# Attention scores as eight independent 64x32 float32 tiles of the TensorE array, instead of split or zero-padded full-array products

## The chip, the cores and the metric

One core of one Trainium2 chip runs the whole program. The metric is device time in microseconds (us) of one execution; three runs of the kernel before gave 707.91, 707.54 and 706.74, median 707.54. The engines are TensorE (PE in the profile, its weight loads PEld), VectorE (DVE), ScalarE (ACT), GpSimd (POOL) and SyncE (SP), which issues most of the DMAs. Each engine works through its own instructions in the order of the built program and waits on semaphores for the others.

## The reference

Eight batches, eight heads, 512 tokens and 32 memory slots per head, head width 64. Both attentions share one score matrix and its transpose; the result goes through a feed-forward layer of 2048 with a squared ReLU.

```python
B, H, S, Ns, D = (8, 8, 512, 32, 64)
scores  = scale * x @ state^T              # (B, H, 512, 32)
a       = softmax(scores);   xread = a  @ state
scores2 = scale * state @ x^T              # the transpose of scores
a2      = softmax(scores2);  sread = a2 @ x
x   = concat([xread, sread], axis=2) -> (B * 544, 512)
out = relu(x @ w_in) ** 2 @ w_out          # d_ff = 2048
```

All of it is float32.

## The kernel before

**The feed-forward part is most of the work.** For each batch the 2048 hidden units are taken in 16 chunks of 128. `mlp` makes for each chunk an `up` (six products of 128x512, tile `ph`, line 392) and a `down` (twelve products, tiles `po`, line 418). The state is folded into `w_in` beforehand: `z` = state times w_in (tile `pz`, line 191 plain, line 203 split), so that `up` multiplies `z` directly with the attention weights `a`. Large products are not done in float32: an operand is split into a high part, rounded to the type `fp32r` (a cast on ScalarE), and a low part (a subtraction on VectorE or GpSimd), both by the helper `split` (lines 97 and 98). Three fp32r products, or two, stand for one in float32.

**The scores of a batch** come in two groups of four heads (`NG` = 2, `HG` = 4). A group has two pairs of heads (`q`). For a pair, 128 rows of `xT` hold both heads' 64 dimensions, and the stationary operand holds the two heads' states in the two diagonal blocks of a matrix that is zero elsewhere, so that one product gives both heads' 32 scores each.

- For the first two batches (`b < PLAIN_X`) the products are plain float32 (line 298): the state is copied into the zeroed `sp_f` (line 250, ScalarE), and two products accumulate into the tile `pst` in PSUM.
- From batch 2 on (line 288), `x` is split into `xt_hl` (`cut_t`: ScalarE, then GpSimd) and the state into `sp_hl` (`pad`: ScalarE, then VectorE). The state's high and low parts stand beside each other as 128 stationary columns, so two products per pair suffice. The lower half of the result (`pq[2N:]`) is copied to SBUF by ScalarE (`st_low`, line 293) and added to the upper half by VectorE (`st`, line 294).

Then both softmaxes run from the scores: a 32x32 transpose and a row maximum on VectorE (lines 303 and 305), the exponentials on ScalarE.

**PSUM.** The pool `ps_x` has two buffers with the tag `px`, for `pst` or `pq`, `pz`, the transposes `pt` and the reads `pr`.

**Products of 64 rows.** At the start of the program TensorE has several plain `pz` products of 64 rows; `pz_361` lies in the array's rows 64 to 127 and `pz_411` in rows 0 to 63:

```order
L191 MATMUL pz_355<-wf_268,st_f_169 128x256 x2
L392 MATMUL ph_231<-a_lo_108,z_hi_232 128x512
L392 MATMUL ph_312<-a_lo_108,z_hi_232 128x512
L191 MATMUL pz_361<-wf_268,st_f_169 128x256 x2
L191 MATMUL pz_411<-wf_285,st_f_169 128x256 x2
```

The two products of `pz_361` stand before the two of `pz_411`; each is two records in the trace.

**What sets the order.** Attention, the `z` products and the weight conversions are cut into steps. `Ahead.run`, called twice per chunk from `mlp`, emits as many steps as their due time asks for; `lags` keeps a step a slot behind what it needs. Within that order a scheduler places the instructions of each engine by its own simulation of the time, so that a step's products may stand apart on TensorE, with `ph` and `po` products between them. The steps of a batch's scores are listed in `order(b)`.

Of the kernel before, what the change touches and what calls it, by code (L numbers as in the profile page):

```python
# [9 lines left out]
F32 = mybir.dt.float32  # L10
F32R = mybir.dt.float32r
# [7 lines left out]
def memory_attention_then_relu2_ffn(  # L19
# [21 lines left out]

    nc = tc.nc
    P = 128
    B, C, S = xT.shape
    D = stT.shape[1]
    H = C // D
    N = stP.shape[2] // (H // 2)
    DM, DF = w_out.shape[1] // 2, w_out.shape[0]
    R = S + N
    NG = H * N // P  # L50
    HG = H // NG
# [5 lines left out]
    FPC = FW // P  # L57
    GB = P // N
    NGB = B // GB
# [1 line left out]
    assert math.frexp(SCALE)[0] == 0.5  # L61
    EPS = 1e-9
    RAW = 4
    XRAW = 2
    PLAIN_Z = 6
    PLAIN_X = 2
    BOTH = ((0, 6), (1, 10), (0, NFC), (1, NFC))
    LATE = 3

# [3 lines left out]
    const = ctx.enter_context(tc.tile_pool(name="const", bufs=1))  # L73
    sb = ctx.enter_context(tc.tile_pool(name="sb", bufs=2))
# [3 lines left out]
    ps_x = ctx.enter_context(tc.tile_pool(name="ps_x", bufs=2, space=bass.MemoryType.PSUM))  # L78
# [2 lines left out]
    make_identity(nc, ident)  # L81

    wo = [None] * NFCH
    sp_hl = const.tile([P, NG, 2, 2, 2 * N], F32R, name="sp_hl")
    nc.gpsimd.memset(sp_hl.bitcast(F32), 0.0)
    sp_f = const.tile([P, NG, 2, P + D], F32, name="sp_f")
    nc.gpsimd.memset(sp_f, 0.0)
    sr = [const.tile([P, C], F32, name=f"sr{i}") for i in range(NGB)]

    wd = [dr.tile([P, NCC, FW], F32, name=f"wd_{k}") for k in range(NFCH)]  # L90
    zd, st, z_first = {}, {}, []
# [31 lines left out]
    def z_state(G):  # L123
        if G == 0:
            raw = sb.tile([P, H, GB * N], F32, name="st_f", tag="x_hl", bufs=1)
            st["raw"] = raw
        else:
            raw = sb.tile([P, H, GB * N], F32, name="st_raw", tag="raw", bufs=RAW)
        for j in range(2):
            nc.sync.dma_start(out=raw[j * D:(j + 1) * D].rearrange("d h m -> d (h m)"), in_=stT[G])  # L130
        hi = sb.tile([P, H, GB * N], F32R, name="stz_hi", bufs=1)
        lo = sb.tile([P, H, GB * N], F32R, name="stz_lo", bufs=1)
        if G:
            split(hi, lo, raw, nc.gpsimd)
# [102 lines left out]


    def attention(b):
        pair = []  # L240

        def pad():
            pair.extend(sb.tile([P, NG, S], F32R, name=n, bufs=2) for n in ("a_hi", "a_lo"))
            raw = sb.tile([P, NG, 2, N], F32, name="sp_raw", bufs=2)
            nc.sync.dma_start(out=raw.rearrange("p g q n -> p (g q n)"), in_=stP[b])
            for i in range(2):
                rows = slice(i * D, (i + 1) * D)
                at = slice(i * N, (i + 1) * N)
                if b < PLAIN_X:
                    nc.scalar.copy(out=sp_f[rows, :, :, at], in_=raw[rows])  # L250
                    continue
                split(sp_hl[rows, :, :, 0, at], sp_hl[rows, :, :, 1, at], raw[rows], nc.vector)

        return pair, pad, [attention_group(b, g, pair) for g in range(NG)]

    def attention_group(b, g, pair):
        CG = C // NG
        NQ = CG // P
        NJ = S // 32
        my = {}  # L260

        def load_t():
            my["t"] = sb.tile([P, NQ, S], F32, name="xt_raw", tag="xraw", bufs=XRAW)
            nc.sync.dma_start(
                out=my["t"], in_=xT[b, g * CG:(g + 1) * CG, :].rearrange("(q p) s -> p q s", p=P)
            )

        def load_n():
            my["n"] = sb.tile([P, NT, CG], F32, name="xn_raw", tag="xraw", bufs=XRAW)
# [1 line left out]
                out=my["n"], in_=xn[b, :, g * CG:(g + 1) * CG].rearrange("(t p) c -> p t c", p=P)  # L271
            )

        def cut_t():
            if b < PLAIN_X:
# [6 lines left out]
        def scores():  # L282
            if b >= PLAIN_X:
                pst = sb.tile([P, S], F32, name="st", bufs=1)
                for q in range(NQ):
                    pq = ps_x.tile([P, S], F32, name="pq", tag="px")
                    for i, v in enumerate(my["xt"]):
                        nc.tensor.matmul(  # L288
                            pq, lhsT=sp_hl[:, g, q].rearrange("p i n -> p (i n)"), rhs=v[:, q, :],
                            start=i == 0, stop=i == 1,  # L290
                        )
# [3 lines left out]
            else:  # L295
                pst = ps_x.tile([P, S], F32, name="pst", tag="px")
                for q in range(NQ):
                    nc.tensor.matmul(
                        pst, lhsT=sp_f[:, g].rearrange("p q n -> p (q n)")[:, q * P:(q + 1) * P],
                        rhs=my["t"][:, q, :], start=q == 0, stop=q == NQ - 1,  # L300
                    )
# [49 lines left out]
        def read():  # L351
# [16 lines left out]
            for q in range(NQ):  # L368
                for i in range(2):
# [4 lines left out]
                        in1=low[i * N:(i + 1) * N, q, i * D:(i + 1) * D],  # L374
                    )

        names = (load_t, cut_t, scores, soft1, soft1b, load_n, cut_n, turn, read)
        return {f.__name__: f for f in names}


# [78 lines left out]
    begins, ends, at = {}, {}, {}  # L459
# [11 lines left out]
    def emit(step):  # L471
        step()
        emitted[step] = slot[0]

    class Ahead:
# [25 lines left out]
    attentions = {b: attention(b) for b in range(B)}  # L501
    a_of = {b: attentions[b][0] for b in range(B)}
    zs = [[z_part(G, k, g) for k in range(NFCH) for g in range(NG)] for G in range(NGB)]
    lags = {}
    for _, _, c, ps in zs[0] + zs[1]:
        lags[ps[0]] = [(c, 2)]
    for b in range(B):
        for g in range(NG):
            w = attentions[b][2][g]
            lags[w["scores"]] = [(w["cut_t"], 1)]  # L510
            lags[w["turn"]] = [(w["scores"], 1)]
            lags[w["read"]] = [(w["turn"], 1), (w["cut_n"], 1)]
            if b:
                lags[w["soft1b"]] = [(w["soft1"], 1)]

    def order(b):
        _, pad, (p, q) = attentions[b]
# [11 lines left out]
    _, pad, (p, q) = attentions[0]  # L529
    z0, z1 = zs  # L530
    for s_ in (
        pad, p["load_t"], q["load_t"], z0[0][0], z0[1][0], p["cut_t"], p["scores"], p["soft1"],
        q["cut_t"], q["scores"], q["soft1"], p["soft1b"], q["soft1b"], lambda: z_state(0),
        z0[0][1], z0[0][2], z0[1][1], z0[1][2], *z0[0][3], *z0[1][3], z0[2][0], z0[3][0],
    ):
        emit(s_)

    weights, reads = Ahead(), Ahead()
    for m in range(NFC):
        steps = []  # L540
# [12 lines left out]
    for m in range(NFC):  # L553
        steps = list(z1[m][3])
# [6 lines left out]
    for b in range(1, B + LATE):  # L561
        steps = order_read(b - LATE) if b >= LATE else []
# [115 lines left out]
```

## Time and profile before

| | |
|---|---|
| runs, median of 3 (lowest to highest) | 707.54 us (706.74 to 707.91) |
| span of the profiled execution | 706.6 us, 9753 instructions |
| TensorE busy | 669.8 us (95%) |
| VectorE / ScalarE / GpSimd busy | 452.2 / 398.3 / 199.3 us |
| DMA | 90.58 MB, mean 128 GB/s |
| chain that ended last | PE 79%, DVE 8%, DMA 6% |

The span is the time from the first to the last instruction of the one profiled execution; the median of the runs is 0.9 us longer. A busy time is the union of an engine's instructions. The ends of matrix products are modelled, so the distance between the starts of two products says what one costs, not the duration in its row. A float32 product stands in the trace as two records, an fp32r product as one. The granted clock (PEclk) is given as a share of 2.4 GHz: 1.00 is that, 0.50 is 1.2 GHz.

### The profile page before, as it was taken

How to read it: one execution, taken by the hardware profiler on the slowest of the kernel's cores; microseconds unless marked ns; L12 is line 12 of the kernel's file. 1: busy time of each engine (PE TensorE's matmuls, PEld its weight loads, DVE VectorE, ACT ScalarE, POOL GpSimd, SP SyncE). 2: the span in 40 equal slices, each digit the busy share in tenths (PEclk: the TensorE clock that was granted, in tenths of full speed). 3: DMA queues.
4: the chain of work that ended last, by engine and by line, in shares of the span. 5: the costliest groups of instructions: out<-in, count | busy, mean ns of one | idle time of the engine just before them, and what ended most of it. 6: DMA issues, size and time to landing. Idle time of an engine off the chain costs nothing.

```text
span 706.6 us, 9753 instructions
## 1 busy us (share of the span) xinstructions
PE 669.8 (95%) x3152; PEld 551.6 (78%) x3152; DVE 452.2 (64%) x757; ACT 398.3 (56%) x727; POOL 199.3 (28%) x181
## 2 busy tenths in 40 slices
PE   4688789999999999999999999999999999999997
PEld 2355668778888888888888878888888888888996
DVE  4859999758456944447945794797944445443553
ACT  3767687567565863467735653665654344332442
POOL 2314433345443540053403240344242022000000
PEclk8589999999999999999999999999999999999999
DMA  8898899435363542344423312412241112100421
GB/s 276 270 315 283 258 306 315 131 97 153 98 202 122 166 149 62 102 135 120 135 78 120 87 48 74 139 58 90 89 150 61 30 31 90 31 16 0 130 80 32
DMA packets 74548, 90.58 MB, mean 128 GB/s; under 512 B 7680, under 2 KB 57600, under 8 KB 74496
## 3 DMA queue, kind: packets, MB, share of 16 engines
q1 hardware_dynamic: 56896, 72.90, 32.9%
q10 hardware_dynamic: 17600, 17.04, 7.1%
q8 instruction: 25, 0.41, 0.3%
q14 instruction: 27, 0.22, 0.1%
HBM read 60.03 MB, written 29.88 MB: 127 GB/s over the span
## 4 chain that ended last, share of the span: by engine, by line
PE 79%; DVE 8%; DMA 6%; issue 2%; ACT 2%; SPq 1%; POOL 0%; DVEq 0%; ACTq 0%; POOLq 0%
PE po L418 47%; PE ph L392 25%; PE pz L203 3%; DMA wo_raw<-w_out 2%; PE pr L355 2%; DMA sp_raw<-stP 2%; PE pq L288 1%; PE pt L343 1%; DVE wf L117 1%; DVE wf L113 1%; DVE z_lo L98 1%; DVE g_lo L98 1%; DMA zd<-z_stage 1%; DMA xt_raw<-xT 1%; DVE wf L109 1%
## 5 line engine op out<-in xcount | busy, mean ns | idle before, releaser
L418 PE MATMUL po<-wo_hi,g_hi 128*128 128x512 f32 x544 | 217.3, 400 | 0.6 <-ACT g_hi L97 0.5
L418 PE MATMUL po<-wo_lo,g_hi 128*128 128x512 f32 x544 | 215.0, 395 | 0.0
L398 DVE TENSOR_TENSOR ph<-ph,r 128x512 f32<-128x512 f32 (+1 forms) x134 | 89.1, 665 | 169.1 <-ACT r L394 168.9
L394 ACT ACTIVATE r<-ph 128x512 f32<-128x512 f32 (+1 forms) x144 | 82.1, 572 | 171.0 <-PE ph L392 169.6
L418 PE MATMUL po<-wo_hi,g_lo 128*128 128x512 f32 x544 | 152.2, 392 | 0.0
L418 PEld LDWEIGHTS po<-wo_hi,g_hi 128*128 128x128 f32 x544 | 103.9, 191 | 22.4 <-ACT g_hi L97 2.0
L418 PEld LDWEIGHTS po<-wo_lo,g_hi 128*128 128x128 f32 x544 | 103.9, 191 | 19.5
L418 PEld LDWEIGHTS po<-wo_hi,g_lo 128*128 128x128 f32 x544 | 101.5, 189 | 21.1 <-issue 1.0
L98 DVE TENSOR_TENSOR g_lo<-ph,g_hi 128x512 fp32r<-128x512 f32 (+1 forms) x144 | 94.4, 656 | 36.3 <-ACT g_hi L97 27.7
L97 ACT CAST g_hi<-ph 128x512 fp32r<-128x512 f32 (+1 forms) x144 | 81.0, 563 | 57.9 <-DVE ph L398 51.7
L392 PE MATMUL ph<-a_hi,z_hi 128*128 128x512 f32 x256 | 81.4, 399 | 2.6 <-DVE nm L306 1.5
L392 PE MATMUL ph<-a_lo,z_hi 128*128 128x512 f32 x256 | 80.1, 392 | 0.0
L392 PE MATMUL ph<-a_hi,z_lo 128*128 128x512 f32 x256 | 80.0, 394 | 0.0
L98 POOL TENSOR_TENSOR xn_hl<-xn_raw,xn_hl 128x1024 fp32r<-128x1024 f32 x16 | 38.9, 2432 | 138.0 <-ACT xn_hl L97 71.2
L182 POOL TENSOR_TENSOR w<-wf,w 64x512 fp32r<-64x512 f32 x32 | 43.0, 1343 | 74.9 <-ACT w L181 69.8
L392 PEld LDWEIGHTS ph<-a_hi,z_hi 128*128 128x128 f32 x256 | 47.6, 190 | 15.2 <-DVE g_lo L98 2.1
L392 PEld LDWEIGHTS ph<-a_hi,z_lo 128*128 128x128 f32 x256 | 48.5, 190 | 10.4
L392 PEld LDWEIGHTS ph<-a_lo,z_hi 128*128 128x128 f32 x256 | 48.2, 189 | 10.5 <-issue 0.3
L98 POOL TENSOR_TENSOR xt_hl<-xt_raw,xt_hl 128x1024 fp32r<-128x1024 f32 x12 | 28.9, 2406 | 75.4 <-ACT xt_hl L97 43.7
L98 DVE TENSOR_TENSOR z_lo<-z_raw,z_hi 128x512 fp32r<-128x512 f32 x64 | 47.9, 750 | 0.3 <-DMA wd<-wf 0.3
L97 ACT CAST z_hi<-z_raw 128x512 fp32r<-128x512 f32 x64 | 39.2, 615 | 1.3 <-DMA wd<-wf 0.8
L98 POOL TENSOR_TENSOR wo_lo<-wof,wo_hi 128x512 fp32r<-128x512 f32 x16 | 25.2, 1578 | 51.4 <-ACT wo_hi L97 51.4
(97 smaller groups left out, 833.7 us busy)
## 6 DMA issues: line engine op xcount, KB each, us to landing
zd<-z_stage ACTq DMA_DIRECT2D x64, 256.0 KB, 3.2
z_raw<-zd SPq DMA_DIRECT2D x252, 64.0 KB, 2.4
xt_raw<-xT SPq DMA_DIRECT2D x16, 512.0 KB, 3.8
w_raw<-w_in SPq DMA_DIRECT2D x16, 512.0 KB, 5.3
wo_raw<-w_out SPq DMA_DIRECT2D x16, 512.0 KB, 5.8
xn_raw<-xn SPq DMA_DIRECT2D x16, 512.0 KB, 3.9
out<-sum SPq DMA_DIRECT2D x32, 256.0 KB, 2.5
wd<-wf SPq DMA_DIRECT2D x16, 256.0 KB, 3.7
```

The costliest lines, as they stand in the source:

```text
L97: nc.scalar.copy(out=hi, in_=src)
L98: eng_lo.tensor_sub(out=lo, in0=src, in1=hi.bitcast(F32))
L109: nc.vector.tensor_scalar(out=bits, in0=bits, scalar1=3, scalar2=0x7FFFFFF8, op0=ALU.logical_shift_left, op1=ALU.bitwise_and,)
L113: nc.vector.scalar_tensor_tensor(out=bits, in0=high, scalar=-0x80000000, in1=bits, op0=ALU.bitwise_and, op1=ALU.bitwise_or,)
L117: nc.vector.scalar_tensor_tensor(out=bits, in0=low, scalar=29, in1=bits, op0=ALU.logical_shift_right, op1=ALU.bitwise_or,)
L182: nc.gpsimd.tensor_sub(out=w[other], in0=wf[own], in1=w[own].bitcast(F32))
L203: nc.tensor.matmul(pz[:, q, :], lhsT=a[:, h, :], rhs=w, start=j == 0, stop=j == len(todo) - 1,)
L355: nc.tensor.matmul(pr[:, q].rearrange("p i c -> p (i c)"), lhsT=my["e"][:, t, q].rearrange("p i n -> p (i n)"), rhs=my["xn"][:, t, q].rear ...
L392: nc.tensor.matmul(ph, lhsT=w, rhs=v, start=i == 0, stop=i == len(todo) - 1)
L394: nc.scalar.activation(r, ph, AF.Relu)
L398: nc.vector.tensor_mul(out=ph, in0=ph, in1=r)
L418: nc.tensor.matmul(po[t], lhsT=g, rhs=w, start=i == 0 and j == 0, stop=i == last and j == 2)
```

## The change

The scores of a batch become one step, `scores`, of eight float32 products. Each has 64 contraction rows and 32 stationary columns, so it takes one of the eight 64x32 tiles of the array: heads 0 to 3 (group 0) lie in partitions 0 to 63, heads 4 to 7 in partitions 64 to 127, and head `j` of a group writes rows `32j` to `32j+31` of that group's `pst`. To allow this, `xT` and `stP` are laid out by halves of heads on the host, as before with other index orders. `pad` only loads the state; `load_a` and `load_b` each load two heads of both halves; `cut_t`, `xt_hl`, `sp_hl`, `sp_f`, `st_low` and `st` are gone. The rest of the old `scores` step is now `exps`, which reads `pst` from PSUM in every batch. `XRAW`, the number of buffers for raw `x`, goes from 2 to 3.

```diff
-    XRAW = 2
+    XRAW = 3
-    sp_hl = const.tile([P, NG, 2, 2, 2 * N], F32R, name="sp_hl")
-    nc.gpsimd.memset(sp_hl.bitcast(F32), 0.0)
-    sp_f = const.tile([P, NG, 2, P + D], F32, name="sp_f")
-    nc.gpsimd.memset(sp_f, 0.0)
...
+        def scores():
+            for g in range(NG):
+                halves[g]["pst"] = ps_x.tile([P, S], F32, name="pst", tag="px")
+            for j in range(HG):
+                x = my["t", j // (HG // 2)][:, j % (HG // 2), :]
+                for g in range(NG):
+                    rows = slice(g * D, (g + 1) * D)
+                    nc.tensor.matmul(
+                        halves[g]["pst"][j * N:(j + 1) * N], lhsT=my["s"][rows, j, :],
+                        rhs=x[rows], start=True, stop=True,
+                    )
...
-        def cut_t():
-            if b < PLAIN_X:
-                return
-            hl = sb.tile([P, 2, NQ, S], F32R, name="xt_hl", tag="x_hl", bufs=1)
-            hi, lo = hl[:, 0], hl[:, 1]
-            split(hi, lo, my["t"], nc.gpsimd)
-            my["xt"] = hi, lo
...
-            if b >= PLAIN_X:
-                pst = sb.tile([P, S], F32, name="st", bufs=1)
-                for q in range(NQ):
-                    pq = ps_x.tile([P, S], F32, name="pq", tag="px")
-                    for i, v in enumerate(my["xt"]):
-                        nc.tensor.matmul(
-                            pq, lhsT=sp_hl[:, g, q].rearrange("p i n -> p (i n)"), rhs=v[:, q, :],
-                            start=i == 0, stop=i == 1,
-                        )
-                    low = sb.tile([2 * N, S], F32, name="st_low", tag="at", bufs=2)
-                    nc.scalar.copy(out=low, in_=pq[2 * N:])
-                    nc.vector.tensor_add(out=pst[q * 2 * N:(q + 1) * 2 * N], in0=pq[:2 * N], in1=low)
...
         return [
-            pad, p["load_t"], p["cut_t"], q["load_t"], p["scores"], p["soft1"], q["cut_t"],
-            q["scores"], p["soft1b"], q["soft1"], q["soft1b"],
+            w["pad"], w["load_a"], w["load_b"], w["scores"], p["exps"], p["soft1"], q["exps"],
+            p["soft1b"], q["soft1"], q["soft1b"],
         ]
```

The order of the instructions changes with it. On TensorE, around the first scores of batch 2, the kernel before has this (`pq` are the scores, `pz` the state times w_in, `po` and `ph` the feed-forward):

```order
L203 MATMUL pz_1499<-w2_1_1359,stz_hi_172 128x256
L288 MATMUL pq_1739<-xt_hl_1710,sp_hl_77 128x512 x2
L418 MATMUL po0_1342<-wo_hi3_520,g_hi_1262 128x512
...
L418 MATMUL po3_1345<-wo_hi3_520,g_lo_1263 128x512
L288 MATMUL pq_1745<-xt_hl_1710,sp_hl_77 128x512 x2
L418 MATMUL po0_1342<-wo_hi3_520,g_hi_1286 128x512
```

and the changed kernel, at the same place, has this:

```order
L198 MATMUL pz_1499<-w2_1_1359,stz_hi_170 128x256
L260 MATMUL pst_1708<-xt_raw_1690,sp_raw_1688 32x512 x2
L260 MATMUL pst_1708<-xt_raw_1706,sp_raw_1688 32x512 x2
L397 MATMUL po0_1342<-wo_hi3_523,g_hi_1262 128x512
...
L397 MATMUL po3_1345<-wo_hi3_523,g_lo_1263 128x512
L260 MATMUL pst_1709<-xt_raw_1690,sp_raw_1688 32x512 x2
L260 MATMUL pst_1709<-xt_raw_1706,sp_raw_1688 32x512 x2
L397 MATMUL po0_1342<-wo_hi3_523,g_hi_1286 128x512
```

The eight tiles of a batch do not stand together: `pst_1708` is group 0, whose four tiles lie in rows 0 to 63 of the array, `pst_1709` is group 1 in rows 64 to 127, and sixteen products on the full array stand between them. Batches 1 to 4 all look so.

In the last batch the eight tiles stand in four places on TensorE. In the changed kernel:

```order
L334 MATMUL pr_4968<-xn_hl_4928,e_hl_4953 128x256
L260 MATMUL pst_5054<-xt_raw_5024,sp_raw_5010 32x512 x2
L260 MATMUL pst_5054<-xt_raw_5040,sp_raw_5010 32x512
L397 MATMUL po0_4285<-wo_hi3_523,g_hi_4494 128x512
...
L260 MATMUL pst_5055<-xt_raw_5024,sp_raw_5010 32x512 x2
...
L260 MATMUL pst_5055<-xt_raw_5040,sp_raw_5010 32x512
L260 MATMUL pst_5054<-xt_raw_5040,sp_raw_5010 32x512
...
L260 MATMUL pst_5055<-xt_raw_5040,sp_raw_5010 32x512
L322 MATMUL pt_5259<-ident_72,e2_3838 128x128 x4
```

where the kernel before has two places of four products each:

```order
L418 MATMUL po3_4392<-wo_hi4_762,g_lo_4668 128x512
L288 MATMUL pq_5215<-xt_hl_5174,sp_hl_77 128x512 x2
L288 MATMUL pq_5221<-xt_hl_5174,sp_hl_77 128x512 x2
L418 MATMUL po0_4389<-wo_hi4_762,g_hi_4706 128x512
...
L288 MATMUL pq_5281<-xt_hl_5265,sp_hl_77 128x512
L288 MATMUL pq_5287<-xt_hl_5265,sp_hl_77 128x512
L288 MATMUL pq_5281<-xt_hl_5265,sp_hl_77 128x512
L288 MATMUL pq_5287<-xt_hl_5265,sp_hl_77 128x512
L418 MATMUL po0_4389<-wo_hi5_913,g_hi_4776 128x512
```

Over batches 2 to 7 the changed kernel has 15 such places: two in each of batches 2 to 4 (4 + 4 tiles), two in batch 5 (7 + 1), three in batch 6 (1 + 1 + 6) and four in batch 7 (3 + 2 + 2 + 1).

On VectorE the two subtractions that make `sp_hl` go in each batch from 2 on; those of batch 2 stood early in the program, among the weight conversions (`wf`).

## Rows read from the trace of the kernel before

**Rows 1.** Busy time of each engine in four stretches (PEclk: granted clock):
```profile
core 0: us, PE busy (x) PEld busy (x) DVE busy (x) ACT busy (x) POOL busy (x), PEclk, DMA share, GB/s
0.00:100.00 100.00, 70.38 (x262) 48.92 (x263) 78.67 (x137) 66.28 (x129) 34.32 (x33) 0.82 0.87 284
100.00:500.00 400.00, 397.90 (x1879) 331.99 (x1879) 273.94 (x453) 244.29 (x437) 139.52 (x116) 1.00 0.40 125
500.00:680.00 180.00, 180.00 (x883) 151.63 (x882) 89.18 (x148) 79.32 (x144) 25.42 (x32) 1.00 0.20 62
680.00:707.00 27.00, 21.55 (x135) 19.09 (x133) 10.37 (x22) 8.38 (x20) 0.00 (x0) 0.98 0.15 41
```
**Rows 2.** What TensorE waited for from 100 us on (us, times, longest):
```profile
PE ph L392 <- DVE g_lo L98: 0.9, 2, 0.6
PE pq L288 <- ACT z_stage L215: 0.7, 1, 0.7
```
**Rows 3.** TensorE at 496 to 498 us (start, duration, what, count):
```profile
496.31 1.07 PE L418 MATMUL po<-wo_hi,g_lo 128*128 128x512 f32 x4
497.21 1.07 PE L288 MATMUL pq<-xt_hl,sp_hl 128*128 128x512 f32 x4
498.12 0.39 PE L418 MATMUL po<-wo_hi,g_hi 128*128 128x512 f32 x1
```
**Rows 4.** Groups by line: line 288 (count, then busy us, mean ns):
```profile
L288 PE MATMUL pq<-xt_hl,sp_hl 128*128 128x512 f32 x48 | 14.6, 391 | 0.7 <-ACT z_stage L215 0.7
```
**Rows 5.** Weight loads of the plain float32 scores at 51 us:
```profile
51.55 0.19 PEld L298 LDWEIGHTS pst<-xt_raw,sp_f 128*128 128x128 f32 x1 [0.24 <-issue]
51.98 0.19 PEld L298 LDWEIGHTS pst<-xt_raw,sp_f 128*128 128x128 f32 x1 [0.24 <-issue]
52.40 0.19 PEld L418 LDWEIGHTS po<-wo_hi,g_lo 128*128 128x128 f32 x1 [0.24 <-issue]
```
**Rows 6.** TensorE at 33 to 40 us, 64-row products among full ones:
```profile
33.37 1.28 PE L191 MATMUL pz<-wf,st_f 64*128 64x256 f32 x4
34.57 0.73 PE L392 MATMUL ph<-a_lo,z_hi 128*128 128x512 f32 x2
35.24 1.21 PE L191 MATMUL pz<-wf,st_f 64*128 64x256 f32 x8
39.11 1.13 PE L191 MATMUL pz<-wf,st_f 64*128 64x256 f32 x4 [2.66 <-ACT z_stage L215]
```
**Rows 7.** Stretches, columns as in Rows 1: the clock at two of these stays:
```profile
35.20:36.40 1.20, 1.20 (x9) 0.81 (x8) 0.00 (x0) 0.07 (x1) 0.96 (x1) 1.00 1.31 232
39.10:40.20 1.10, 1.09 (x4) 0.67 (x4) 1.03 (x3) 1.10 (x3) 0.00 (x0) 1.00 1.00 401
```
**Rows 8.** Timeline of VectorE, the state's split near the start:
```profile
18.79 1.33 DVE L98 TENSOR_TENSOR sp_hl<-sp_raw,sp_hl 64x128 fp32r<-64x128 f32 x2
```
**Rows 9.** The start as one stretch, columns as in Rows 1:
```profile
9.30:35.00 25.70, 14.40 (x44) 8.31 (x42) 22.88 (x45) 16.71 (x36) 7.88 (x7) 0.60 0.87 280
```
**Rows 10.** Chain of waits, 9 to 35 us, two pieces (start, us, what):
```profile
6.14 10.32 DMA sp_raw<-stP
...
17.20 3.78 DMA sp_raw<-stP
```
**Rows 11.** Groups by line that the change removes on the other engines:
```profile
L98 POOL TENSOR_TENSOR xt_hl<-xt_raw,xt_hl 128x1024 fp32r<-128x1024 f32 x12 | 28.9, 2406 | 75.4 <-ACT xt_hl L97 43.7 <-issue 31.8
L294 DVE TENSOR_TENSOR st<-pq,st_low 64x512 f32<-64x512 f32 x24 | 16.4, 682 | 3.1 <-ACT st_low L293 2.8
L293 ACT COPY st_low<-pq 64x512 f32<-64x512 f32 x24 | 13.7, 583 | 7.0 <-PE pq L288 6.8
L97 ACT CAST xt_hl<-xt_raw 128x1024 fp32r<-128x1024 f32 x12 | 12.6, 1048 | 4.5 <-DMA xt_raw<-xT 2.3 <-PE pr L355 2.2
```
**Rows 12.** The page's DMA issues: loads of x (KB, us to landing):
```profile
xt_raw<-xT SPq DMA_DIRECT2D x16, 512.0 KB, 3.8
```

More of the change, by code (lines that the diff above doesn't have):

```diff
@@ L43, in memory_attention_then_relu2_ffn @@
     P = 128
-    B, C, S = xT.shape
+    B, S, C = xn.shape
     D = stT.shape[1]
     H = C // D
-    N = stP.shape[2] // (H // 2)
+    N = stT.shape[2] * stT.shape[0] // (B * H)
     DM, DF = w_out.shape[1] // 2, w_out.shape[0]
@@ L63, in memory_attention_then_relu2_ffn @@
     RAW = 4
-    XRAW = 2
+    XRAW = 3
     PLAIN_Z = 6
-    PLAIN_X = 2
     BOTH = ((0, 6), (1, 10), (0, NFC), (1, NFC))
@@ L239, in attention, with load_t, run, attention_group @@
     def attention(b):
-        pair = []
+        pair, my = [], {}
+        halves = [{} for _ in range(NG)]
         def pad():
             pair.extend(sb.tile([P, NG, S], F32R, name=n, bufs=2) for n in ("a_hi", "a_lo"))
[L244 to L248, printed above, removed]
-                if b < PLAIN_X:
[L250 to L256, printed above, removed]
+            my["s"] = sb.tile([P, HG, N], F32, name="sp_raw", bufs=2)
+            nc.sync.dma_start(out=my["s"].rearrange("p j n -> p (j n)"), in_=stP[b])
+        def load_t(i):
+            def run():
+                js = slice(i * HG // 2, (i + 1) * HG // 2)
+                t = sb.tile([P, HG // 2, S], F32, name="xt_raw", tag="xraw", bufs=XRAW)
+                nc.sync.dma_start(
+                    out=t, in_=xT[b].rearrange("p (j s) -> p j s", j=HG)[:, js, :]
+                )
+                my["t", i] = t
+            return run
+        def scores():
[8 more added lines that the diff above has]
+                        rhs=x[rows], start=True, stop=True,
+                    )
+        steps = dict(pad=pad, load_a=load_t(0), load_b=load_t(1), scores=scores)
+        return pair, steps, [attention_group(b, g, pair, halves[g]) for g in range(NG)]
+    def attention_group(b, g, pair, my):
         CG = C // NG
@@ L259, in attention_group @@
         NJ = S // 32
[L260 to L265, printed above, removed]
-            )
         def load_n():
@@ L272, in load_n, with exps @@
             )
-        def cut_t():
-            if b < PLAIN_X:
-                return
-            hl = sb.tile([P, 2, NQ, S], F32R, name="xt_hl", tag="x_hl", bufs=1)
-            hi, lo = hl[:, 0], hl[:, 1]
-            split(hi, lo, my["t"], nc.gpsimd)
-            my["xt"] = hi, lo
-        def scores():
-            if b >= PLAIN_X:
-                pst = sb.tile([P, S], F32, name="st", bufs=1)
-                for q in range(NQ):
-                    pq = ps_x.tile([P, S], F32, name="pq", tag="px")
-                    for i, v in enumerate(my["xt"]):
-                        nc.tensor.matmul(
-                            pq, lhsT=sp_hl[:, g, q].rearrange("p i n -> p (i n)"), rhs=v[:, q, :],
-                            start=i == 0, stop=i == 1,
-                        )
-                    low = sb.tile([2 * N, S], F32, name="st_low", tag="at", bufs=2)
-                    nc.scalar.copy(out=low, in_=pq[2 * N:])
-                    nc.vector.tensor_add(out=pst[q * 2 * N:(q + 1) * 2 * N], in0=pq[:2 * N], in1=low)
[L295 to L301, printed above, removed]
+        def exps():
+            pst = my["pst"]
             q1 = sb.tile([P, NJ, N], F32, name="q1", bufs=2)
@@ L375, in read @@
                     )
-        names = (load_t, cut_t, scores, soft1, soft1b, load_n, cut_n, turn, read)
+        names = (exps, soft1, soft1b, load_n, cut_n, turn, read)
         return {f.__name__: f for f in names}
@@ L509, in memory_attention_then_relu2_ffn @@
             w = attentions[b][2][g]
-            lags[w["scores"]] = [(w["cut_t"], 1)]
-            lags[w["turn"]] = [(w["scores"], 1)]
+            lags[w["exps"]] = [(attentions[b][1]["scores"], 1)]
+            lags[w["turn"]] = [(w["exps"], 1)]
             lags[w["read"]] = [(w["turn"], 1), (w["cut_n"], 1)]
@@ L516, in order @@
     def order(b):
-        _, pad, (p, q) = attentions[b]
+        _, w, (p, q) = attentions[b]
         return [
-            pad, p["load_t"], p["cut_t"], q["load_t"], p["scores"], p["soft1"], q["cut_t"],
-            q["scores"], p["soft1b"], q["soft1"], q["soft1b"],
+            w["pad"], w["load_a"], w["load_b"], w["scores"], p["exps"], p["soft1"], q["exps"],
+            p["soft1b"], q["soft1"], q["soft1b"],
         ]
@@ L527, in order_read @@
         ]
-    _, pad, (p, q) = attentions[0]
+    _, w, (p, q) = attentions[0]
     z0, z1 = zs
     for s_ in (
-        pad, p["load_t"], q["load_t"], z0[0][0], z0[1][0], p["cut_t"], p["scores"], p["soft1"],
-        q["cut_t"], q["scores"], q["soft1"], p["soft1b"], q["soft1b"], lambda: z_state(0),
+        w["pad"], w["load_a"], w["load_b"], z0[0][0], z0[1][0], w["scores"], p["exps"], p["soft1"],
+        q["exps"], q["soft1"], p["soft1b"], q["soft1b"], lambda: z_state(0),
         z0[0][1], z0[0][2], z0[1][1], z0[1][2], *z0[0][3], *z0[1][3], z0[2][0], z0[3][0],
@@ L653 @@
     arrays = {
-        "xT": np.ascontiguousarray(x.transpose(0, 1, 3, 2)).reshape(B, H * D, S),
+        "xT": np.ascontiguousarray(
+            x.reshape(B, 2, H // 2, S, D).transpose(0, 1, 4, 2, 3)
+        ).reshape(B, 2 * D, H // 2 * S),
         "xn": np.ascontiguousarray(x.transpose(0, 2, 1, 3)).reshape(B, S, H * D),
@@ L659 @@
         "stP": np.ascontiguousarray(
-            state.reshape(B, H // 2, 2, N, D).transpose(0, 2, 4, 1, 3)
+            state.reshape(B, 2, H // 2, N, D).transpose(0, 1, 4, 2, 3)
         ).reshape(B, 2 * D, H // 2 * N),
```

## The prediction

> **What bounds the kernel now.** I read the busy times by stretch first. From 100 us to 680 us TensorE is busy 577.9 of 580 us at the full clock; in the first 100 us it is busy 70.4 us, beside VectorE with 78.7 us and DMA engines that are 87% busy [rows 1]. So there are two regimes. In the long one each microsecond added to TensorE is a microsecond of the result, and what the other engines save is worth nothing: TensorE waits for them 2.1 us in all, 0.7 us of it before a score product [rows 1, 2]. In the first 100 us VectorE's conversions and the transfers set the pace, and TensorE has 29.6 us to spare. Batches 0 and 1 are scored in the second kind of stretch, batches 2 to 7 in the first. Next I looked up what the scores cost TensorE (the timeline around line 288), and what a float32 product and a 64-row tile cost (lines 298 and 191).
>
> **What the change takes away on TensorE.** In batches 2 to 7 there are 48 score products [rows 4]. Four of them take from 497.21 to 498.12 us, 0.91 us, or 0.2275 us each, as the four feed-forward products ahead do (496.31 to 497.21) [rows 3]. 48 x 0.2275 = 10.9 us, all in the regime where TensorE is full. They also need no change of the array's form: every product there is 128 x 128.
>
> **What it adds.** Six batches of eight float32 products with 512 columns. A float32 product is two records, and the weight loads of two such records stand 0.43 us apart (51.55, 51.98, 52.40) at the full clock [rows 5], so one takes 0.853 us (four times 512 columns at 2.4 GHz). Done one after the other, eight are 6.8 us, against 1.8 us for the eight fp32r products they replace. The change pays only if tiles run beside each other.
>
> Do they? The trace has tiles of 64 rows in line 191. Four records on one row half take 1.13 us (39.11); eight records, four on each half, take 1.21 us (35.24), both at the full clock [rows 6, 7]. So the two halves do run side by side, although the program has both products of one half before both of the other. No product of the kernel before has fewer than 128 columns, so tiles that share rows and differ in columns are not shown. And that is what the change needs: in batches 2 to 4 a place holds four tiles of the same 64 rows. From below a place costs one product's 0.853 us, from above one product for each tile of the fuller row half. I take the lower end, since the nearest row, the 64-row tiles, shows full overlap; the upper end is a rival.
>
> The Trainium skill weighs in here twice. The page "TensorE: Matmul & The Clock Gate", in Part 3 on what overlaps, says that products start and end strictly in program order; the 64-row rows above contradict it, since the second half would have had to wait for the third record of the first. What the rule would do to this kernel is a rival below. The same Part has a measurement for column tiles, which no run here shows: three of them with 512 columns were 2.38 times as fast as in turn, so that, by an estimate from it, a place of three or four tiles would cost about a quarter more and the sum would be some 2 us higher.
>
> **The change of form.** Going into the 64-row form and back costs time too. The stay of four records at 33.37 lasts to the next product's start at 34.57, 1.20 us, where four records stream for 0.853; two full products then last to 35.24, 0.67 us, where two take 0.455 [rows 6, 3]. That is 0.35 + 0.22 = 0.57 us for the way in and out; part of the first is at the lower clock (0.60 on average over this start [rows 9]), so I take 0.50 us, with 0.35 to 0.57 as the range.
>
> How often? The order of the changed kernel has 15 separate places of tiles in batches 2 to 7. In each, the longest chain on one tile is one product, whether the place holds one tile or seven. So 15 x (0.853 + 0.50) = 20.3 us. Against the 10.9 us removed, TensorE has **9.4 us more** in the regime where it is full. Even with no price on the form it is 15 x 0.853 = 12.8, 1.9 us more: the scheduler's spreading eats the parallelism. With all eight tiles in one place it would have been 6 x 1.35 = 8.1 us, a gain of 2.8.
>
> **The other engines.** GpSimd loses 28.9 us (`xt_hl`), VectorE 16.4 (`st`), ScalarE 13.7 and 12.6 [rows 11]. After 100 us TensorE covers them, and had it not, 2.1 us is all that it waited for. The first softmax instructions now read `pst` in PSUM, in both `px` buffers at once, but the next user of `px` on TensorE stands 19 or more products later (over 4 us) nearly everywhere, and the transpose and maximum there need about as long as the copies and sums they replace. I cost that at nothing; without cover it is a wait of about one such instruction (0.68 us) a batch, 4 us.
>
> **The start.** VectorE is busy 22.88 of 25.70 us between 9.3 and 35 us [rows 9], and 1.33 us of it, the split of batch 2's state, goes [rows 8]. Because VectorE sets the pace, that is worth up to 1.33 us; ScalarE's copies of the same state, on which the chain of waits stands (it counts 10.32 us to that transfer's landing [rows 10]), go too. What is late next is VectorE's own conversions, so the gain can't be over 1.33 plus VectorE's idle 2.82 us, 4.15 us; from below it is nothing, or a loss if the transfers, merely reordered, set the pace. I take 1.5 us. The faster scores of batches 0 and 1 fall where TensorE waits anyhow, and count nothing. The x bytes are the same: 16 loads of 512 KB [rows 12].
>
> **Sum.** Against the profiled execution's span of 706.6 us: 706.6 + 9.4 - 1.5 = 714.5. The median of the runs is 0.9 us over that span, which lies around it and stays: **715.4 us**, 1.1% slower. Its own range: 15 x 1.20 = 18.0 and a gain of 4.15 at the start give 710.5; 15 x 1.42 = 21.3 and no gain give 717.9.
>
> **Rivals.**
> - *Column tiles take turns.* If tiles of one row half share a stream, a place costs its fuller half: 8 products in each of batches 2 to 4, then 5, 5 and 7, together 41 x 0.853 = 35.0, with the changes of form (7.5) 42.5, less 10.9 is 31.6 more: 737.6 us. For it: no row shows column tiles. Against: the row halves overlap freely.
> - *Records start strictly in order.* The second record of a tile needs its first, and the next tile may start only beside that second one: a place of n tiles costs (n + 1) x 0.427. The 15 places hold 48 tiles, 63 x 0.427 = 26.9, plus 7.5, less 10.9: 23.5 more, 729.5 us. The rule on program order in Part 3 of the Trainium skill's page "TensorE: Matmul & The Clock Gate" is this mechanism. Against it stands the overlap at 35.24 [rows 6].
> - *The start gains more than TensorE loses (other side).* The chain of waits puts 14.1 us of the first 21 on the landing of the state's small transfers [rows 10], and ScalarE and VectorE, which waited there in order, no longer do. If that was the real hold and not an early prefetch, a gain of 12 us gives 705; it decides from 9.4 us on, or from 1.9 if the form costs nothing. Against: VectorE has 2.82 us of idle time to give there, and 12 us in the whole first 100 [rows 1].
> - *TensorE waits for x.* Formerly ScalarE waited for the loads (2.3 us in all [rows 11]); now a late load stops TensorE and every feed-forward product behind it. A load lands 3.8 us after issue [rows 12]; half of that in each of six batches is 11 us more, 727.
>
> **Chances.** The forecast 0.62; turns 0.06; strict order 0.08; waiting for x 0.08; the start's gain, with a form that is nearly free, 0.16. Of the last, 0.12 is faster by over 0.2% (what a measurement of this kernel can tell from no change) and 0.04 within it; with a tail of the forecast I say faster 0.12, same 0.06, slower 0.82. The range 706 to 724 leaves out the two rivals of columns, most of the waits for x, and the better half of the start's gains.
>
> **What would show it.** Right: line 260 on TensorE in 15 places after 100 us; tiles of one place starting within a few tens of ns; about 1.35 us from a place's start to the next feed-forward product's steady pace; TensorE as full as before between 100 and 680 us; the start some 1.5 us earlier. Wrong: starts of the tiles of one place 0.43 or 0.85 us apart (strict order, or turns); TensorE waiting for `xt_raw`; a place that costs under 1.0 us; or the steady regime beginning many us earlier than now.

## The result, and the profile after

The change makes the kernel slower: 718.44 us median (716.68 to 720.58 in 4 runs) against 707.16 us (706.74 to 707.91), a ratio of 1.0145 with a 95% interval of 1.0122 to 1.0169. The forecast was 715.4 us, with a range of 706 to 724. The profiled execution took 720.58 us, the longest of the four, and its span is 718.8 us, 12.2 us over the span before. Three executions of the experiments below ran at a far lower granted clock (one of the kernel before at 0.835, one of "joined" at 0.566, and the profiled one of "x held" at 0.667) and are left out.

The same four stretches as in [rows 1], after the change (columns as there: PE, PEld, DVE, ACT, POOL, granted clock, DMA share, GB/s):

```profile
0.00:100.00 100.00, 60.04 (x255) 42.09 (x256) 79.60 (x133) 59.69 (x112) 35.26 (x31) 0.90 0.83 276
100.00:500.00 400.00, 395.50 (x1901) 318.47 (x1901) 242.05 (x405) 218.45 (x393) 112.55 (x105) 1.00 0.40 126
500.00:680.00 180.00, 180.00 (x856) 148.99 (x855) 91.96 (x150) 76.28 (x138) 23.57 (x31) 1.00 0.18 56
680.00:719.00 39.00, 33.67 (x210) 30.04 (x208) 16.97 (x35) 14.22 (x34) 0.00 (x0) 0.98 0.21 60
```

The time is lost twice. In the first 100 us TensorE is busy 10 us less (60.0 against 70.4; a part of that is the higher granted clock, 0.90 for 0.82). From 100 to 680 us it is nearly as full as before (575.5 of 580 us, 577.9 there), but 33.67 us of work are left at 680 us where there were 21.55. What it waited for from 100 us on, against [rows 2]:

```profile
PE ph L371 <- DVE g_lo L93: 2.5, 3, 1.1
PE pz L198 <- ACT z_stage L210: 1.4, 1, 1.4
PE po L397 <- ACT g_hi L92: 0.5, 1, 0.5
```

No wait for `xt_raw` stands there, nor one of line 260: the scores themselves are never late in the steady regime.

One mark separates the two losses in every kernel below: the start of the 240th `po` product (counted from 0, in order of start). It stands at 168.0 us before and at 175.1 after, so 7.1 us are lost up to there and 5.1 us of the 12.2 behind it.

Now a place of tiles, for [rows 3]. TensorE around the six tiles (twelve records) of one place of batch 6 (start, duration, what, count):

```profile
455.14 0.39 PE L371 MATMUL ph<-a_hi,z_lo 128*128 128x512 f32 x1
455.37 0.61 PE L371 MATMUL ph<-a_lo,z_hi 128*128 128x512 f32 x2
455.91 1.08 PE L260 MATMUL pst<-xt_raw,sp_raw 64*32 64x512 f32 x12
456.92 0.50 PE L397 MATMUL po<-wo_hi,g_hi 128*128 128x512 f32 x1
457.25 0.39 PE L397 MATMUL po<-wo_lo,g_hi 128*128 128x512 f32 x1
457.48 0.40 PE L397 MATMUL po<-wo_hi,g_hi 128*128 128x512 f32 x1
```

Products on the full array start 0.23 us apart. The last one ahead of the place starts at 455.59, 0.32 us before the first tile, so 0.09 over the pace; the place itself lasts 1.01 us; the step behind it (456.92 to 457.25) is 0.335, 0.11 over the pace. Together 1.20 us for six products. The same place cut into three stretches, its `pst` records alone, shows how they start (the column PE has the count of records under way):

```profile
455.90:455.95 0.05, 0.04 (x6) 0.04 (x8) 0.00 (x0) 0.00 (x0) 1.00 0.76 246
455.95:456.35 0.40, 0.40 (x6) 0.13 (x12) 0.00 (x0) 0.00 (x0) 1.00 1.04 399
456.35:456.42 0.07, 0.07 (x12) 0.00 (x0) 0.00 (x0) 0.00 (x0) 1.00 1.00 380
```

All six tiles are under way within 50 ns (single records start 7 ns apart), and their six second records join between 456.36 and 456.40, 0.45 us later. This holds for tiles of the same rows and of different rows alike. A place with one tile (batch 6) and one with four (batch 3):

```profile
441.24 1.04 PE L260 MATMUL pst<-xt_raw,sp_raw 64*32 64x512 f32 x2
442.21 0.50 PE L397 MATMUL po<-wo_hi,g_hi 128*128 128x512 f32 x1
442.55 0.40 PE L397 MATMUL po<-wo_lo,g_hi 128*128 128x512 f32 x1
...
234.91 1.06 PE L260 MATMUL pst<-xt_raw,sp_raw 64*32 64x512 f32 x8
235.90 0.50 PE L397 MATMUL po<-wo_hi,g_hi 128*128 128x512 f32 x1
236.23 0.39 PE L397 MATMUL po<-wo_lo,g_hi 128*128 128x512 f32 x1
```

From the first tile to the next full product it is 0.97 us with one tile, 0.99 with four, 1.01 with six. Counted by the single starts from the product before to the second one after, less two at the pace, a place costs 1.17 us with one tile, 1.19 with four and 1.22 with eight: a nearly fixed price, 1.19 below, and the tiles in it are nearly free.

In the start, what TensorE waited for up to 150 us (the largest rows, first of the kernel before, then of the one after; us, times, longest):

```profile
PE pz L191 <- DVE wf L117: 11.7, 4, 4.0
PE pst L298 <- DMA xt_raw<-xT: 4.9, 1, 4.9
PE pz L191 <- ACT z_stage L215: 2.7, 1, 2.7
PE pz L203 <- ACT w L97: 2.5, 2, 2.2
```
```profile
PE pz L198 <- ACT z_stage L210: 9.7, 4, 3.6
PE pz L186 <- DMA xt_raw<-xT: 9.3, 1, 9.3
PE pst L260 <- DMA xt_raw<-xT: 6.6, 1, 6.6
PE po L397 <- ACT g_hi L92: 5.9, 2, 5.4
PE pz L186 <- ACT wf L103: 5.5, 1, 5.5
PE pst L260 <- ACT z_stage L210: 3.5, 1, 3.5
```

With the smaller rows the waits grow from 31 us to 44, and most of them are on weights being converted, on `x` or on `z` (`z_stage` is its copy out of PSUM; `g_hi` and `g_lo` are the split squares of the hidden units). The last load of `w_out` is issued 5 us later (before, then after: shortest, median and longest issue in ns, then the first and the last start in us):

```profile
L444 SPq DMA_DIRECT2D wo_raw<-w_out x16: 328/377/666, 21.3 to 117.7; - x16
```
```profile
L423 SPq DMA_DIRECT2D wo_raw<-w_out x16: 328/384/447, 21.9 to 122.7; - x16
```

A load of `x`, 3.8 us from issue to landing in [rows 12], now takes 5.1 in the median:

```profile
xt_raw<-xT SPq DMA_DIRECT2D x16, 512.0 KB, 5.1
```

### The profile page after: what moved, and what is told of

It is laid out like the page before. It is cut to its first block, busy times and chain, and to the rows that moved or that the text cites. A ratio compares the mean times of both kernels' runs of the same rounds, so it can differ in the third digit from the quotient of the medians.

```text
span 718.8 us, 9769 instructions
## 1 busy us (share of the span) xinstructions
PE 669.2 (93%) x3216; PEld 539.6 (75%) x3216; DVE 430.6 (60%) x721; ACT 368.6 (51%) x675; POOL 171.4 (24%) x167
## 4 chain that ended last, share of the span: by engine, by line
PE 80%; DMA 8%; DVE 6%; issue 2%; ACT 2%; SPq 1%; POOL 0%; ACTq 0%; DVEq 0%
PE po L397 48%; PE ph L371 25%; PE pst L260 2%; PE pz L198 2%; PE pr L334 2%; DMA w_raw<-w_in 2%; DMA wo_raw<-w_out 2%; DMA z_raw<-zd 1%; DMA st_f<-stT 1%; DMA zd<-z_stage 1%; PE pt L322 1%; DVE wf L108 1%; DMA xt_raw<-xT 1%; DVE wf L112 1%; DVE wof L108 1%
## 5 line engine op out<-in xcount | busy, mean ns | idle before, releaser
L93 DVE TENSOR_TENSOR z_lo<-z_raw,z_hi 128x512 fp32r<-128x512 f32 x64 | 50.0, 783 | 0.0
L93 POOL TENSOR_TENSOR wo_lo<-wof,wo_hi 128x512 fp32r<-128x512 f32 x16 | 27.1, 1694 | 66.7 <-ACT wo_hi L92 66.7
L210 ACT COPY z_stage<-pz 128x512 f32<-128x512 f32 x64 | 37.3, 585 | 8.7 <-PE pz L198 6.9
```

The source lines that it names most:

```text
L210: nc.scalar.copy(out=stage, in_=pz)
```

## Experiments

Two theories to begin with. *Places*: the steady loss is the number of places times 1.19 us, less the 10.9 us of products removed, whatever stands in a place. *Start*: the new early scores gain about what the prediction said, and what they lose comes with the third `x` buffer, through which loads of later batches enter the start. The rival to the second: the order of the start decides, whichever edit caused it. All kernels below ran beside the kernel before (medians 707.77 to 708.45 us there). In the table the places are those after 100 us; "240th" is how much later than before that `po` product starts in the profiled execution; "rest" is what the span lost behind it.

| kernel | median us | ratio to before [95%] | places | 240th | rest |
|---|---|---|---|---|---|
| the change | 718.44 | 1.0145 [1.0122, 1.0169] | 15 | +7.1 | +5.1 |
| late | 714.57 | 1.0085 [1.0060, 1.0110] | 15 | +2.2 | +5.8 |
| late, two buffers | 716.49 | 1.0120 [1.0101, 1.0139] | 15 | +0.5 | +8.0 |
| early | 707.44 | 0.9981 [0.9967, 0.9996] | 0 | -1.7 | +0.1 |
| two buffers | 712.84 | 1.0068 [1.0044, 1.0092] | 14 | -2.4 | +9.4 |
| critical section | 721.06 | 1.0184 [1.0158, 1.0210] | 6 | +11.7 | 0.0 |
| x held | 714.76 | 1.0094 [1.0074, 1.0114] | 15 | | |
| xn held | 714.91 | 1.0101 [1.0077, 1.0124] | 15 | +3.7 | +5.8 |
| joined, two buffers | 703.49 | 0.9930 [0.9908, 0.9952] | 9 | -6.2 | -0.3 |
| joined | 708.90 | 1.0014 [0.9996, 1.0032] | 10 | -1.9 | +2.4 |
| joined, x held | 713.62 | 1.0077 [1.0056, 1.0098] | 11 | +3.9 | +1.7 |
| joined, xn held | 710.60 | 1.0037 [1.0018, 1.0056] | 11 | -0.2 | +3.2 |
| joined, both held | 708.07 | 1.0006 [0.9989, 1.0023] | 10 | -0.1 | +1.6 |

**Late and early: half of the change each.** The scores of only some batches are tiles; the others keep the old code, and their x and state the old layout. Late keeps three buffers, early has two.

```diff
+    NEW = range(2, 8)     # late;  early: range(0, 2)
...
+            if b in NEW:
+                pst = my["pst"]
+            elif b >= PLAIN_X:
+                pst = sb.tile([P, S], F32, name="st", bufs=1)
...
```

> New tiles in batches 2 to 7 alone; batches 0 and 1 are scored as before. Theory of places: each separate place of tiles costs TensorE about 1.19 us whatever it holds, as the trace of the change has it, and there are again 15 places after 100 us, so 15 x 1.19 - 10.9 = 6.9 us over before, 714 us, with a start as long as before. Rival (the start's loss does not come from the first two batches' scores but from the third buffer for x, which this kernel has too): 7 + 5, 719 us.

> New tiles in batches 0 and 1 alone, two buffers for x; batches 2 to 7 are scored as before. Theory that the first two batches' new scores lengthen the start: about 5 us over before, 712 us, with the last of VectorE's weight conversions some 5 us later. Rival (the start's loss comes from the buffers or from elsewhere): within 2 us of before, 705 to 709 us.

Late lost 6.1 us (714.57 against 708.45), of it +5.8 behind the 240th product; early gained 1.0, of it 1.7 at that product and nothing behind it. The steady loss belongs to the tiles of batches 2 to 7, and tiles in batches 0 and 1 are not a loss by themselves. The 7 us that the change lost in the start are not the sum of the two.

**Two buffers.** The change with `XRAW` left at 2.

```diff
-    XRAW = 3
+    XRAW = 2
```

> The change with two buffers for raw x instead of three. 14 places of tiles after 100 us instead of 15. Theory that the first two batches' scores lengthen the start: as the change less one place, 717 us. Rival (the third buffer lets loads of x in ahead of the weights): the start's loss of about 5 us goes, 712 us.

It takes back half of the loss: ratio 1.0068 for 1.0145, 5.4 us, and the 240th product comes 2.4 us early where it was 7.1 late. The start's loss hangs on the third buffer. The rest is larger than in the change, 9.4 us, with one wait of 2.2 us for `g_hi` at 456 us in it.

**Critical section.** The eight products of a batch in one, so that nothing can come between.

```diff
-            for j in range(HG):
+            with tc.tile_critical():
+              for j in range(HG):
```

> The change, with the eight products of a batch kept together on TensorE: one place a batch, six after 100 us. Theory of places (a fixed price for each, about 1.2 us, whatever it holds): 9 places fewer, 10.7 us less than the change, 708 us. Rival (tiles share something, and eight together cost clearly more than four): a place of eight takes 1.7 to 2 us and the gain is 6 to 7 us, 712 us.

A miss. There are six places as wanted, and the rest behind the 240th product is 0.0, but each place costs more, and the start loses 11.7 us. The first tile of batch 0 starts at 16.94 us, where the change waited 6.6 us for `x`:

```profile
PE pst L261 <- DMA xt_raw<-xT: 16.9, 1, 16.9
```

That the section holds its first product until all of it can start is the likely reason; no run shows it apart. TensorE around the place of batch 7:

```profile
470.63 0.61 PE L398 MATMUL po<-wo_hi,g_lo 128*128 128x512 f32 x2
471.68 1.09 PE L261 MATMUL pst<-xt_raw,sp_raw 64*32 64x512 f32 x16 [0.43 <-ACT z_hi L92]
472.92 0.49 PE L372 MATMUL ph<-a_hi,z_hi 128*128 128x512 f32 x1
```

The queue waits ahead of the section: 1.05 us from 470.63 to the first tile, where two products and the step into the form need 0.54, so 0.5 us more. From the first tile to the next product it is 1.24 us where a place of eight needs 1.02 (below). That is 0.7 us for each of the five places behind the mark, 3.7 in all (the one of batch 6 waited 0.13 longer). Taken off, the rest is -3.7; 5 places at 1.19 less 40 removed products at 0.2275 are -3.2.

**Joined: fewer places without a section.** The product whose `x` is loaded last is issued first; the other seven stand behind it in issue order and at a higher priority. Run with two buffers and with three.

```diff
+            last = one(HG - 1, NG - 1)
+            with tc.issue_after(last.ins), tc.high_priority():
+                for j in reversed(range(HG)):
+                    for g in reversed(range(NG)):
+                        if (j, g) != (HG - 1, NG - 1):
+                            one(j, g)
```

> Two x buffers, and the eight products of a batch are asked to follow one another (the one whose x comes last stands first, the others at a higher priority behind it): 9 places after 100 us in place of 14 or 15. Theory (the price is per place, 1.19 us whatever the number of tiles): 9 x 1.19 = 10.7 us against 10.9 us removed, steady about -0.2 us, start -2 us, so about 706.5 us against 708.45 before and 712.84 for the two-buffer version in 15 places. Rival (the price is per product, or the scores cost what they cost however they are grouped): as the two-buffer version, 712 to 715 us.

> Three x buffers with no hold, the eight products asked to follow one another: 10 places after 100 us. Theory: 10 x 1.19 = 11.9 us less 10.9 us = +1.0 us, start +7 us as in the change, so about 716 us, and the 240th po product some 7 us late. Rival (what the start lost in the change came from the early scores being spread over the weight conversions, not from the third buffer): about 707 us, the 240th po product 1 to 3 us early.

Both came out faster than the first theory of each said, and with two buffers the kernel is faster than the one before: 703.49 us, 0.9930 [0.9908, 0.9952]. One of its places with all eight tiles:

```profile
221.03 0.39 PE L403 MATMUL po<-wo_hi,g_lo 128*128 128x512 f32 x1
221.35 1.09 PE L259 MATMUL pst<-xt_raw,sp_raw 64*32 64x512 f32 x16
222.37 0.50 PE L403 MATMUL po<-wo_hi,g_hi 128*128 128x512 f32 x1
222.70 0.39 PE L403 MATMUL po<-wo_lo,g_hi 128*128 128x512 f32 x1
```

1.02 us to the next product, so eight tiles cost what six do. And the stretches of [rows 1] in this kernel:

```profile
0.00:100.00 100.00, 71.66 (x291) 49.92 (x292) 79.91 (x141) 64.86 (x124) 30.58 (x31) 0.88 0.86 281
100.00:500.00 400.00, 399.46 (x1957) 326.50 (x1956) 256.94 (x436) 221.55 (x400) 116.54 (x110) 1.00 0.40 128
500.00:680.00 180.00, 180.00 (x884) 152.03 (x883) 82.96 (x133) 74.50 (x139) 19.38 (x26) 1.00 0.19 59
680.00:700.10 20.10, 15.02 (x91) 13.08 (x89) 6.79 (x14) 5.88 (x14) 0.00 (x0) 0.95 0.10 26
```

The steady part is level with before, as forecast (rest -0.3; 8 places behind the mark at 1.19 less 9.1 make +0.4). The gain is the start, -6.2 us where -2 was expected. With three buffers the start is -1.9 us: that is the rival's number, not the +7 of the theory. Yet beside its twin with two buffers the third one costs again, 1.0014 against 0.9930, 5.9 us, of which one more place explains 1.2. So both the order of the early scores and the buffer are in it.

**Which load is it?** The third buffer lets the first `x` of batch 2 be issued at 13.4 us (two buffers: 48.6; joined with two: 40.7) and the first `xn` of batch 0 at 50.3 (150.9; 148.4). Such loads were held back, by an edge of issue order alone, behind the last load of `w_out`: batch 2's `x`, then batch 0's `xn`, then `xn` there and `x` behind the fifth load of `w_out`.

```diff
+                if b == 2:
+                    tc.add_manual_dep(
+                        load.ins, last_weight[-1].name,
+                        mybir.DependencyInfo(
+                            mybir.DependencyClass.NoSync, mybir.DependencyReason.DATA
+                        ),
+                        reason="behind the weights",
+                    )
```

> The change with its third x buffer kept, but batch 2's two x loads are issued behind the last load of w_out, so that they cannot come into the start. Its scores stand in 15 places after 100 us, as the change's own. Theory (the start loses because the third buffer draws loads of later batches in among the weights, and 15 places at 1.19 us net less 10.9 us of removed products cost the rest): steady +6.9 us, start -1.5 to -2.5 us as with two buffers, so about 713 us against 708.45 for the kernel before, and the 240th po product 1 to 3 us earlier than before. Rival (the start loses by the third buffer's order in itself, not by those early loads): 717 to 720 us, the 240th po product some 7 us late as in the change.

> Three x buffers, batch 2's x loads held behind the last load of w_out, and the eight products asked to follow one another: 11 places after 100 us. Theory (start by the early loads, steady by the number of places): 11 x 1.19 = 13.1 us less 10.9 us = +2.2 us, start -2 us, so about 708.6 us. Rival 1 (the start loses by the third buffer in itself): about 716 us. Rival 2 (the number of places does not matter): about 713 us.

> As the joined three-buffer version (709.34 us, two more than before), but the loads of batch 0's xn stand behind the last load of w_out; batch 2's first x load stays early (some 15 us). 11 places after 100 us, so steady 11 x 1.19 - 10.9 = +2.2 us. Theory A (what the third buffer costs in the start is the early xn: its loads of 512 KB and its rounding on ScalarE and GpSimd at about 60 us): start as in the joined two-buffer version, some 5 to 6 us early, so about 704.5 us against 708 before. Theory B (it is the early x load): start as in the joined three-buffer version, about 709.5 to 710 us.

> As that, and batch 2's two x loads stand behind the fifth load of w_out, where the joined two-buffer version has them (some 41 to 44 us): the third buffer is there, the loads come in the order of two buffers. 10 places after 100 us, steady +1.0 us. Theories A and B: start some 5 to 6 us early, about 703.5 us. Theory C (the third buffer costs in some other way): 708 to 710 us.

> The change itself (three buffers, 15 places after 100 us, steady +6.9 us) with only the loads of batch 0's xn held behind the last load of w_out. Theory A: the start as in the two-buffer version (level with before), about 714 to 715 us. Theory B: as the change, 718 to 720 us.

None of these forecasts fits all of it. In the order of the change, holding `x` gave back 3.6 us (1.0094 for 1.0145) and holding `xn` 3.1 (1.0101). In the joined order, holding `x` lost 4.5 us and holding `xn` 1.6 (one more place explains 1.2 of each). Holding both gained 0.6, which is within the intervals, and stayed 5.4 us behind the joined version with two buffers. So theories A and B fall as they stand: no hold gives all of the start back.

They do not clear the early loads, though, since a hold moves a load and does not restore the order of two buffers. Up to 115 us the held joined versions are about as early as the joined one with two buffers (the 120th `po` product 5.2 us early with `xn` held, 5.1 with both, 4.1 with `x`, 4.5 there; 1.9 with three buffers and no hold). They lose their 5 us or more from there to 140 us. In that stretch come the last weights, and now the held loads as well: `xn` of batch 0 is issued at 116 to 140 us, where two buffers have it at 148.4 and 149.6. TensorE from 108 to 142 us (joined with two buffers, then "xn held", then "both held", columns as above):

```profile
108.00:142.00 34.00, 34.00 (x166) 28.65 (x165) 25.99 (x37) 20.81 (x39) 10.82 (x8) 1.00 0.65 205
108.00:142.00 34.00, 30.73 (x147) 24.31 (x146) 29.41 (x39) 21.71 (x39) 13.29 (x9) 1.00 0.84 263
108.00:142.00 34.00, 29.90 (x139) 23.34 (x138) 28.99 (x38) 21.54 (x39) 14.07 (x9) 1.00 0.77 240
```

In the joined versions without a hold no `xn` is loaded there and TensorE is full, with two buffers and with three. Three buffers with `xn` held to some 148 us would tell more; there is no such run.

**Late, two buffers.** The last test of the buffer: the late version, with old scores in batches 0 and 1, and `XRAW` 2 for 3.

> As the version with the tiles in batches 2 to 7 only (old scores in batches 0 and 1; 714.57 us against 708.45 before, ratio 1.0085), but with two x buffers in place of three; again 15 places after 100 us, steady some +6 to +7 us. Theory (the third buffer costs 5 to 6 us in the start, whatever the scores there look like, as the change against its two-buffer version and the joined pair showed): about 709 us, ratio 1.000 to 1.002, the 240th po product 3 to 4 us early. Rival (the third buffer costs that much only together with the new scores of batches 0 and 1): 713 to 715 us, ratio 1.007 to 1.010.

The rival was right about the start: with two buffers it gained 1.75 us (240th +0.5 for +2.2), not 5 to 6. The time is above even the rival's range, 716.49 us, and not better than with three buffers (1.0120 for 1.0085, intervals that overlap a little). The rest is 2.2 us larger, and 3.1 us of waits for `g_hi` stand behind the mark, at 232 and 459 us (those for `g_lo` stand ahead of it):

```profile
PE po L443 <- ACT g_hi L96: 3.1, 2, 1.6
PE ph L417 <- DVE g_lo L97: 2.0, 2, 1.2
```

## Why the prediction was right, and where it was not

**TensorE sets the pace from 100 to 680 us: right.** It is nearly as full as before, and every other engine's saving there was worth nothing.

**48 products removed, 10.9 us: right.** With no tiles after 100 us (early) the rest is +0.1; with them it follows the places. Behind the mark 40 old products (9.1 us) go, and places at 1.19 us make +6.4 for the change (13 places; measured +5.1), +7.6 for late (14; +5.8), +7.6 for "xn held" (14; +5.8), +0.4 for joined with two buffers (8; -0.3), +1.6 for the joined ones with three (9; +1.6 to +3.2). The two kernels far off contain waits: the two-buffer one (13 places, +6.4; measured +9.4 with 2.2 of waits over 1 us), late with two buffers (13, +6.4; +8.0, with 3.1). The joined ones with three have 1.6 us of waits behind the mark, where the kernel before has 0.8. The rest of the spread, up to 1.8 us, is partly in the mark: up to 1.5 us of `pz`, `pt` and `pr` products stand ahead of it that stood behind it before.

**Column tiles overlap fully: right.** The rivals in which they take turns or start in strict order are out: starts 7 ns apart within a place, 0.97 us for one tile and 1.02 for eight. The page "TensorE: Matmul & The Clock Gate" of the Trainium skill, in Part 3, has three column tiles 2.38 times as fast as in turn. By the prediction's estimate from it a place of three or four would have cost a quarter more. No such cost is in these rows.

**The price of a place, 1.35 us: mis-sized.** It is 1.19, since the way into the form and back costs 0.34 us (1.19 less 0.853), not 0.50. The stay of 64-row products it was read from, 33.37 to 34.57 us [rows 6], stood at a mean granted clock of 0.85 (33.30 to 34.60), where the places after 100 us have 1.00. The term 15 x 1.35 - 10.9 = +9.4 should have been 15 x 1.19 - 10.9 = +7.0.

**The start, -1.5 us: wrong, for this kernel.** The gain is there when the edit stands alone (early: -1.7 at the mark), so the reason given was fair. What failed is how the third buffer was costed, by its bytes only ("The x bytes are the same"): the prediction allowed a loss "if the transfers, merely reordered, set the pace" and gave it no number. With the early tiles it costs 9.5 us at the mark in the order of the change (+7.1 against -2.4) and 4.3 in the joined order (-1.9 against -6.2); with the old early scores 1.7. On medians the start of the change lost about 4.3 us (11.3 in all less 7.0), where -1.5 stood. The two errors, -2.4 and +5.8, have opposite signs, and so, in part by luck, the forecast came within 3.0 us of the result (the other 0.4 is the median of before, 707.16 here and 707.54 there).

**The other rivals.** TensorE waits for no `x` after 100 us. The start did not gain more; the prediction's remark there, that VectorE had 12 us of idle in the first 100, was a slip: 100 less 78.67 is 21.3.

**What stays open** is why the third buffer costs what it does. It depends on the order of the early scores, and whether it lies in where the early loads stand is not decided by the holds. One thing the traces do show is a price that moves with the order. Two engines of the change at 60 us:

```profile
61.67 2.56 POOL L93 TENSOR_TENSOR xn_hl<-xn_raw,xn_hl 128x1024 fp32r<-128x1024 f32 x1
```
```profile
60.71 1.27 DVE L104 TENSOR_SCALAR wf<-wf 128x512 int32<-128x512 int32 x1
62.02 2.75 DVE L108 SCALAR_TENSOR_TENSOR wf<-w_raw,wf 128x512 int32<-128x512 int32 x1
```

Line 108 on VectorE takes 0.69 us in the median for the same shape, and 2.75 here: it starts while GpSimd's rounding of `xn` runs (to 64.23) and ends 0.54 us after it. Every VectorE instruction of the first 135 us that took over 0.15 us more than the median of its kind overlapped one of GpSimd's, in all thirteen profiles (all but that of "x held"): 280 instructions, of which 278 ended 0.03, 0.28 or 0.55 us after a GpSimd instruction that had started before them. Not every overlap does it: 209 others that started with over 0.3 us of a GpSimd instruction to go were not slowed, among them each `g_lo`, which reads PSUM. The excess of the slowed ones sums to 17.6 us before, 19.8 in the change, 14.6 with two buffers, 14.7 joined with two buffers; so 5.2 us lie between the change and its two-buffer version, which are 9.5 apart at the mark. But joined with three buffers has 14.6 too and starts 4.3 us later than with two, and the late versions have 21.1 to 21.7 with starts near +1. So it may be a part of the cost; no experiment of its own tests it. The Trainium skill's page "SBUF — State Buffer", under "SBUF: two separate sides", says that GpSimd and some VectorE instructions share a pair of ports as an exclusive lock, the later one waiting for the whole of the earlier. The rows above agree.

## What to carry to other kernels

Count the places in the order that the scheduler really makes, not the products: small tiles of the array run beside each other at almost no cost (0.05 us for seven more), but each separate stay in the tiled form costs its full length (1.19 us here), so that the scores in 15 places cost 5 to 6 us more than the old products (waits aside) and in 9 about the same. An edit of buffers that is neutral in bytes is not neutral in a start that several engines and queues bound together: test it apart from the edit it came with. And keep the edit that pays: tiles with two buffers and the products joined run in 703.49 us, 0.7% faster than the kernel before.

## What was not expected of the hardware

- Tiles in different columns of the same rows start 7 ns apart, and a float32 product's second record follows its first after 453 ns (none to seven others between them); eight tiles stretch a place by 0.05 us over one.
- A stay in the tiled form costs 0.34 us beside its streaming, of which 0.09 lies ahead of the first tile and 0.11 behind the first full product.
- A section that keeps eight products together costs TensorE 0.5 us ahead of it and 0.2 behind it.
- Some VectorE instructions that start beside a running GpSimd one end only 0.03, 0.28 or 0.55 us after it, so that 0.69 us becomes 2.75; others, such as `g_lo`, are not slowed.
